# The last four frequencies turned inside SBUF, 15 late products behind the last stage, and the io ring in another room

## The chip, the core and the metric

The kernel runs on one core of one Trainium2 chip, in float32 (some operands of the dense products split into two fp32r halves). The metric is the device time of one execution in microseconds (us). Before the change the median of three runs is 531.04 us (530.05 to 533.01). The profiled execution is one more execution, 531.73 us long.

## The reference

Two branches over the same 2048 rows of 512 channels are mixed by a gate for each row. The first is a long convolution of `u` with a kernel K that is built from 128 complex modes for each channel (S4), done by Fourier transforms; the second is a dense layer with GELU and a second dense layer. Cut to what is computed:

```python
g = sigmoid((u * gate_w).sum(-1, keepdims=True))
P = exp(logdA[:, :, None] * l)                  # l = 0..2047
K = einsum("dn,dnl,dn->dl", Cc, P, dB).real
Y = rfft(pad(u)) * rfft(pad(K))                 # along the 2048 rows, padded to 4096
a = irfft(Y)[:2048] + u * Dskip
b = gelu(x @ w1 + b1) @ w2 + b2                 # 512 -> 1792 -> 512
out = g * a + (1 - g) * b
```

## The kernel before

The program has two parts. `front()` runs from 0 to about 408 us: it builds K, does the first stage of both Fourier transforms, and most of the dense layers; a planner with costs and due times sets its order. It stores the dense part of the outputs into the output tensor in DRAM (`out_dram`) from a ring of three tiles, `io`; the last two of these stores are accumulating stores on POOL's queue (L947). What is left of the second dense layer, 14 triples of matmuls (42, onto two accumulators `acc` for the last two of the 16 row tiles), is handed on as the list `late`.

`conv()` is the second part, in an order written out by hand. The long transform is split as 32 x 64: 32 outer frequencies n, each with 64 inner ones in real and imaginary parts on the 128 partitions. A loop over s = 0 to 15 takes two outer frequencies at a time. In each step:

- `fetch` loads two tiles `tk` (256 KB each, eight buffers) from DRAM on SP's queue, and `load_u` the like of the signal into buffers in `attic` and `loft`;
- `product(s)` multiplies the two spectra on DVE in six instructions (L1118 to L1123) into tiles `v`;
- `signal(s+1)` and `taps(s+2)` do the second transform stage of the coming steps on PE (L1096, into `p2u` and `p2k`), and ACT copies `p2k` to `k`;
- `inverse(s)` does the first stage back on PE (L1135, into `pa`, 8 matmuls for a step);
- `turn(s)` copies `pa` to a tile `sa` (ACT, L1141, six buffers) and stores it to DRAM in `t4_d` (L1144), on SP's queue but for the last, which goes on ACT's. An `sa` tile has 128 partitions in the order (q, i, c): 32 values of q, two halves i, real and imaginary c. With the eighth frequency of a group the whole group is loaded back into `t3` (L1153), turned so that the frequencies lie along the partitions: groups 0 to 2 in four loads of 512 KB each on POOL's queue, the last one in eight of 256 KB, four on ACT's and four on SP's;
- for s = 6 to 13 `dense(s-6)` loads 512 KB of the dense part of the output back into SBUF (L1163, SP).

In SBUF each tile has its room, and a tile that takes a room over waits for what used it last. `t3`, `tk`, `v` and the rest of `conv()` lie in rooms that `front()` used.

Behind the loop stand the remaining late products (`rest`, L1174 to L1176; one triple stands ahead of the last inverse), a warm matmul (L1212), two sums of the late accumulators into the outputs on DVE (L1216), and the last stage: 128 matmuls `pb` from `t3` (L1224), of which each pair of row tiles m = 0 to 7 takes 16. The gated sum into the output tile is done on DVE (L1235, eleven tiles) or on ACT and POOL (L1232, L1233, five tiles), and the output tiles are stored (L1237 one tile, L1239 two).

Of the kernel before, what the change touches and what calls it, by code (L numbers as in the profile page):

```python
# [9 lines left out]
F32 = mybir.dt.float32  # L10
# [62 lines left out]
N_PASS = 20  # L73
N_LATE = 2

N_ATTIC, N_LOFT, N_TK = 11, 8, 8
N_US = N_ATTIC + N_LOFT
W_DVE = ((1, 0), (3, 0), (5, 0))

GROUP = 8  # L80

ASIDE = (2, 4, 7, 9, 12)
# [24 lines left out]
def constants():  # L107
# [26 lines left out]
    f2 = np.zeros((32, 2, 64, 64))  # L134
    g2 = np.zeros((32, 64, 64, 2))
    for n, k in enumerate(ko):
        er, ei = om(4 * (q[:, None] * k + 32 * np.outer(q, k1)) + q[:, None])
        f2[n, 0], f2[n, 1] = er, -ei
        er, ei = om(4 * (qn[None] * k + 32 * np.outer(k1, qn)) + qn[None])
        g2[n, :, :, 0], g2[n, :, :, 1] = er, -ei  # L140
    f2 = f2.reshape(8, 4, P, 64).transpose(0, 2, 1, 3).reshape(8, P, 256)
# [149 lines left out]
def gated_mix(  # L291
# [23 lines left out]
    dt_d = dr.tile([1, D], F32, name="dt_d")  # L315
    t4_d = dr.tile([4, 2, 2, GROUP, 32, D], F32, name="t4_d")
    tu_d = dr.tile([2, 32, 2, 64, D // 2], F32, name="tu_d")
# [30 lines left out]
    def front(pool, psum, keep, attic, loft):  # L348
# [3 lines left out]
        def tiles(n, shape, nm, dtype=F32, space=pool):  # L352
            return [space.tile(shape, dtype, name=f"{nm}{k}") for k in range(n)]
# [25 lines left out]
        y = pool.tile([P, 2, 64, CW], F32, name="y")  # L379
        xc = tiles(2, [P, 2, 32, CW], "xc")  # L380
        xt_, xv_ = (loft[:, k * 1024 : k * 1024 + 1024].rearrange("p (a b c) -> p a b c", a=2, c=CW) for k in range(2))
        tt = loft[:, 2048:4160].rearrange("p (a b c) -> p a b c", a=2, c=CW)
# [19 lines left out]

        io = tiles(N_IO, [P, D], "io")
        gs = pool.tile([P, 16], F32, name="gs")
# [650 lines left out]
    def conv(pool, ps, late, attic, loft):  # L1055
# [17 lines left out]
        def matrices(m):  # L1073

            cc = c4s[m]
            f = cc[:, 0].rearrange("p (n k) -> p n k", n=4)
            f1 = pool.tile([P, 4, 64], F32, tag="f1", name=f"f1{m}", bufs=2)
            g = cc[:, 1].rearrange("p (s q c) -> p s q c", s=2, c=2)
            g1 = pool.tile([P, 2, 64, 2], F32, tag="g1", name=f"g1{m}", bufs=2)
            nc.scalar.mul(f1[0:64], f[64:128], -1.0)  # L1080
            nc.scalar.copy(f1[64:128], f[0:64])
            nc.scalar.mul(g1[:, :, :, 0], g[:, :, :, 1], -1.0)
            nc.scalar.copy(g1[:, :, :, 1], g[:, :, :, 0])
            mats[m] = (f, f1), [z.rearrange("p s q c -> p s (q c)") for z in (g, g1)]

# [51 lines left out]
        def turn(s):  # L1137

            for n in (2 * s, 2 * s + 1):
                sa = sas[n % 6]  # L1140
                nc.scalar.copy(sa, pas.pop(n))  # L1141
                g, k = divmod(n, GROUP)
                on = nc.sync if n < 31 else nc.scalar
                on.dma_start(t4_d[g, :, :, k].rearrange("i c q d -> q (i c) d"), sa)  # L1144
                if k < GROUP - 1:
                    continue
                rows = t4_d[g].rearrange("i c k q d -> (i c k) q d")


                w = 8 if n < 31 else 4  # L1150
                for h in range(0, 32, w):
                    on = nc.gpsimd if n < 31 else (nc.scalar, nc.sync)[h // w % 2]
                    on.dma_start(t3[g:P:4, h : h + w], rows[:, h : h + w])  # L1153

# [34 lines left out]
        for s in range(16):  # L1189
# [16 lines left out]
            if 6 <= s < 14:  # L1206
                dense(s - 6)
        rest(14)

        warm = ps.tile([P, D], F32, tag="pa", name="warm", bufs=2)  # L1210
        for _ in range(N_KEEP):
            nc.tensor.matmul(warm[0:64], mats[7][0][1][:, 3], zs[0], start=True, stop=True)  # L1212
        for s in range(N_LATE):
            z = mos[7][:, s]
            a = accs[NT - N_LATE + s]
            nc.vector.scalar_tensor_tensor(z, a, gate[:, 1, 14 + s : 15 + s], z, ALU.mult, ALU.add)  # L1216

        for m in range(8):
            tag, n = ("pa", 2) if m % 3 == 2 else ("pu", 4)
            pbs = [ps.tile([P, D], F32, tag=tag, name=f"pb{m}{i}", bufs=n) for i in range(2)]  # L1220
            for b in range(4):
                for i in range(2):
                    r = slice(64 * i, 64 * i + 64)
                    nc.tensor.matmul(  # L1224
                        pbs[i][32 * b : 32 * b + 32], g1t[r], t3[r, 4 * m + b], start=True, stop=True
                    )
            for i in range(2):
                t = 2 * m + i
                z, g = mos[m][:, i], gate[:, 0, t : t + 1]
                if t in ASIDE:  # L1230
                    a = sas[ASIDE.index(t)]
                    nc.scalar.mul(a, pbs[i], g)  # L1232
                    nc.gpsimd.tensor_add(z, z, a)  # L1233
                else:
                    nc.vector.scalar_tensor_tensor(z, pbs[i], g, z, ALU.mult, ALU.add)  # L1235
                if m in (0, 7):
                    (nc.sync, nc.scalar)[i if m else 0].dma_start(ov[m, :, i], z)  # L1237
            if 0 < m < 7:
                nc.sync.dma_start(ov[m], mos[m])  # L1239

    ctx.enter_context(tc.manual_schedule())
# [76 lines left out]
```

## Time and profile before

| | us |
|---|---|
| median of three runs | 531.04 (530.05 to 533.01) |
| the profiled execution | 531.73 |
| its span | 529.9 |
| PE busy | 502.9 (95%) |
| DVE busy | 425.5 (80%) |
| ACT busy | 348.2 (66%) |
| POOL busy | 47.5 (9%) |
| first product of `conv()` on DVE starts at | 416.54 |
| first `pb` matmul starts at | 512.97 |

The span reaches from the first to the last instruction of the profiled execution; the execution's own time is 1.83 us longer. A busy engine is one that executes an instruction; the time that DMA transfers take is not in these rows, but in a share of the 16 DMA engines and in the time from a transfer's issue to its landing. In a timeline row the bracket at the end tells how long the engine stood idle before it, and what released it. Where a row stands for several instructions (x4), its second number is the time from the first one's start to the last one's end.

### The profile page before, as it was taken

What the parts mean: (1) busy time and instruction counts of PE and PEld (TensorE: products, weight loads), DVE (VectorE), ACT (ScalarE), POOL (GpSimd) and SP (SyncE); (2) the same over time, 40 slices, a digit from 0 to 9 for tenths busy, and PEclk for the clock granted to TensorE, in tenths of its full rate; (3) what the DMA queues carried; (4) which work ended last, traced back from release to release, by engine and by line L of the source; (5) the groups of instructions that cost most, each with busy time, mean ns of one, the idle gap of its engine ahead of it and who ended that gap; (6) DMA issues with size and microseconds to landing.
All of it is one profiled execution on the core that took longest, in us unless ns stands there. A gap on an engine that the chain in (4) does not pass through costs nothing.

```text
span 529.9 us, 11252 instructions
## 1 busy us (share of the span) xinstructions
PE 502.9 (95%) x4426; PEld 348.7 (66%) x4426; DVE 425.5 (80%) x790; ACT 348.2 (66%) x539; POOL 47.5 (9%) x90
## 2 busy tenths in 40 slices
PE   8998999999999889999999999899999899999992
PEld 4776788778787666788787787688777233333360
DVE  5899999989999897899999896999801467666533
ACT  5899868599975976977459947666544355555311
POOL 1000000000000030002200320031101001010104
PEclk9999999999999989999999999999999899999997
DMA  8999932471499286426670533483718979999877
GB/s 228 380 349 329 352 133 82 143 236 32 145 292 296 64 248 203 164 79 175 126 180 1 155 46 41 111 209 42 186 47 216 287 254 299 382 406 386 324 274 294
DMA packets 90836, 108.60 MB, mean 205 GB/s; under 512 B 39056, under 2 KB 58576, under 8 KB 90144
## 3 DMA queue, kind: packets, MB, share of 16 engines
q1 hardware_dynamic: 82944, 87.67, 50.1%
q0 software_dynamic: 7360, 18.65, 14.2%
q10 hardware_dynamic: 480, 1.57, 0.8%
q8 instruction: 35, 0.57, 0.5%
q14 instruction: 17, 0.14, 0.1%
HBM read 62.25 MB, written 45.62 MB: 204 GB/s over the span
## 4 chain that ended last, share of the span: by engine, by line
PE 38%; DVE 22%; DMA 16%; issue 8%; ACT 8%; SPq 5%; POOL 1%; POOLq 0%; ACTq 0%; DVEq 0%
PE pa L1135 6%; PE p2u L1096 5%; PE p2k L1096 4%; DMA tk_d<-sk 4%; PE pz L707 4%; PE ph L876 4%; PE ph L877 3%; PE ph L878 3%; DMA tu_d<-attic 3%; PE acc L922 3%; SPq L746 3%; DVE loft L517 3%; DVE y L671 3%; DVE loft L516 3%; PE acc L923 2%
## 5 line engine op out<-in xcount | busy, mean ns | idle before, releaser
L876 PE MATMUL ph<-xh,wh 128*128 128x512 f32 x224 | 89.2, 398 | 2.9 <-ACT io L895 2.1
L922 PE MATMUL acc<-wh,hh 128*128 128x512 f32 x210 | 85.4, 406 | 3.9 <-ACT acc L928 3.9
L877 PE MATMUL ph<-xlo,wh 128*128 128x512 f32 x224 | 87.6, 391 | 0.4 <-DVE xlo L810 0.4
L878 PE MATMUL ph<-xh,wl 128*128 128x512 f32 x224 | 87.4, 390 | 0.0
L923 PE MATMUL acc<-wl,hh 128*128 128x512 f32 x210 | 82.2, 391 | 0.0
L924 PE MATMUL acc<-wh,hl 128*128 128x512 f32 x210 | 82.1, 391 | 0.0
L707 PE MATMUL pz<-y,xc 128*32 128x64 f32 x2048 | 62.5, 291 | 5.3 <-ACT attic L451 2.5
L707 PEld LDWEIGHTS pz<-y,xc 128*32 128x32 f32 x2048 | 57.1, 137 | 12.4 <-ACT sk L727 3.7
L904 DVE TENSOR_TENSOR hl<-io,hh 128x512 fp32r<-128x512 f32 x56 | 38.4, 685 | 27.2 <-ACT hh L896 27.2
L895 ACT ACTIVATE io<-ph,b1t 128x512 f32<-128x512 f32 x56 | 38.6, 689 | 26.0 <-PE ph L878 23.3
L876 PEld LDWEIGHTS ph<-xh,wh 128*128 128x128 f32 x224 | 42.0, 188 | 17.2 <-ACT io L895 3.4
L922 PEld LDWEIGHTS acc<-wh,hh 128*128 128x128 f32 x210 | 39.4, 187 | 21.1 <-issue 8.4
L877 PEld LDWEIGHTS ph<-xlo,wh 128*128 128x128 f32 x224 | 42.1, 188 | 9.4 <-DVE xlo L810 1.1
L878 PEld LDWEIGHTS ph<-xh,wl 128*128 128x128 f32 x224 | 42.1, 188 | 9.0
L924 PEld LDWEIGHTS acc<-wh,hl 128*128 128x128 f32 x210 | 39.4, 188 | 9.1 <-DVE hl L904 0.5
L671 DVE TENSOR_TENSOR y<-y,ea 128x64 f32<-128x64 f32 (+4 forms) x80 | 45.0, 563 | 0.2
L923 PEld LDWEIGHTS acc<-wl,hh 128*128 128x128 f32 x210 | 39.5, 188 | 7.3
L936 ACT ACTIVATE io<-acc,gate 128x512 f32<-128x512 f32 x30 | 20.6, 687 | 29.5 <-PE acc L924 28.7
L516 DVE TENSOR_TENSOR loft<-xc,zz 128x256 f32<-128x256 f32 (+2 forms) x48 | 37.1, 772 | 3.3 <-ACT xc L642 3.1
L1118 DVE TENSOR_TENSOR v<-p2u,k 128x512 f32<-128x512 f32 x16 | 11.1, 691 | 34.5 <-ACT sa L1141 23.6
L684 DVE TENSOR_TENSOR y<-y,loft 128x2048 f32<-128x2048 f32 x16 | 36.6, 2285 | 0.9 <-ACT loft L634 0.8
L517 DVE TENSOR_TENSOR loft<-xc,zz 128x256 f32<-128x256 f32 (+2 forms) x48 | 37.0, 771 | 0.0
(139 smaller groups left out, 845.2 us busy)
## 6 DMA issues: line engine op xcount, KB each, us to landing
tu_d<-attic SPq DMA_DIRECT2D x16, 512.0 KB, 5.9
tk_d<-sk SPq DMA_DIRECT2D x16, 512.0 KB, 6.5
tk<-tk_d SPq DMA_DIRECT2D x32, 256.0 KB, 6.0
t_d<-sa SPq DMA_DIRECT2D x31, 256.0 KB, 5.1
t<-t_d POOLq DMA_DIRECT2D x12, 512.0 KB, 7.1
attic<-tu_d SPq DMA_DIRECT2D x22, 256.0 KB, 4.6
attic<-in_xt_dram SPq DMA_DIRECT2D x16, 256.0 KB, 4.6
attic<-in_xl_dram SPq DMA_DIRECT2D x16, 256.0 KB, 5.1
```

Source lines behind the costliest of these rows:

```text
L516: vec(2 * m, lambda: vv.tensor_mul(t, a, br), due, [ka, *kb], [kt])
L517: vec(2 * m, lambda: vv.tensor_mul(v, a, bi), due, [ka, *kb], [kv])
L671: nc.vector.tensor_mul(both(n, 64 - 3 * n, n), both(0, 64 - n, n), an)
L707: nc.tensor.matmul(pk[32 * j : 32 * j + 32, gg // 4, gg % 4], x[:, r, :, ch], y[:, r, :, ch], start=(r == 0), stop=(r == 1), skip_group_ch ...
L876: nc.tensor.matmul(phs[q], h, xh[d], start=(d == 0), stop=False)
L877: nc.tensor.matmul(phs[q], h, xlo[d], start=False, stop=False)
L878: nc.tensor.matmul(phs[q], lo, xh[d], start=False, stop=(d == 3))
L895: nc.scalar.activation(g, phs[q], AF.Gelu_apprx_tanh, bias=b1t[:, c : c + 1])
L922: nc.tensor.matmul(a, h, wh[1][f], start=(f == 0 and u >= NSB), stop=False, skip_group_check=True)
L923: nc.tensor.matmul(a, h, wl[1][f], start=False, stop=False, skip_group_check=True)
L924: nc.tensor.matmul(a, l, wh[1][f], start=False, stop=(f == FH - 1), skip_group_check=True)
L1096: nc.tensor.matmul(out[64 * i : 64 * i + 64], w, x, start=True, stop=True)
```

## The change

It has three parts.

1. **The turn.** The constants of the inverse stage are laid out anew so that an `sa` tile has the partition order (i, c, q) instead of (q, i, c). The stores of n = 0 to 23 go to `t4_d`, with the pattern 4x32x512 in place of 32x4x512. Those of n = 24 to 27 go to a new DRAM tile `t5_d` with rows of 528 instead of 512 values, and come back in four loads of 256 KB on POOL's queue. Frequencies 28 to 31 aren't stored: one transfer each, three on SP's queue and one on ACT's, copies `sa` straight to four partitions of `t3`. The eight loads of the last group and four stores are gone.
2. **The late products.** Ahead of the last stage `rest` takes eight triples, and the others stand behind the `pb` matmuls of the last pair of row tiles; the two sums of the late accumulators stand behind them on DVE, and the two output tiles concerned are stored last, one on SP's queue and one on ACT's.
3. **The io ring.** `io` is allocated further ahead, and so lies in room that `t3` has later, no longer in the room that the first `v` tiles have.

```diff
@@ constants() @@
-    g2 = np.zeros((32, 64, 64, 2))
+    g2 = np.zeros((32, 64, 2, 2, 32))
...
-        g2[n, :, :, 0], g2[n, :, :, 1] = er, -ei
+        for i in range(2):
+            g2[n, :, i, 0], g2[n, :, i, 1] = er[:, i::2], -ei[:, i::2]
@@ gated_mix() @@
+N_FIRST = 8
+LATE = L // P - N_LATE
-    t4_d = dr.tile([4, 2, 2, GROUP, 32, D], F32, name="t4_d")
+    t4_d = dr.tile([3, 2, 2, GROUP, 32, D], F32, name="t4_d")
+    t5_d = dr.tile([2, 2, GROUP // 2, 32, D + 16], F32, name="t5_d")
@@ front() @@
         xc = tiles(2, [P, 2, 32, CW], "xc")
+        io = tiles(N_IO, [P, D], "io")
...
-        io = tiles(N_IO, [P, D], "io")
         gs = pool.tile([P, 16], F32, name="gs")
@@ matrices() @@
-            g = cc[:, 1].rearrange("p (s q c) -> p s q c", s=2, c=2)
-            g1 = pool.tile([P, 2, 64, 2], F32, tag="g1", name=f"g1{m}", bufs=2)
+            g = cc[:, 1].rearrange("p (s i c q) -> p (s i) c q", s=2, i=2, c=2)
+            g1 = pool.tile([P, 4, 2, 32], F32, tag="g1", name=f"g1{m}", bufs=2)
...
-            nc.scalar.mul(g1[:, :, :, 0], g[:, :, :, 1], -1.0)
-            nc.scalar.copy(g1[:, :, :, 1], g[:, :, :, 0])
+            nc.scalar.mul(g1[:, :, 0], g[:, :, 1], -1.0)
+            nc.scalar.copy(g1[:, :, 1], g[:, :, 0])
@@ turn() @@
-                on = nc.sync if n < 31 else nc.scalar
-                on.dma_start(t4_d[g, :, :, k].rearrange("i c q d -> q (i c) d"), sa)
+                if n >= 28:
+                    on = nc.sync if n < 31 else nc.scalar
+                    on.dma_start(t3[g + 4 * k : P : 32], sa)
+                    continue
+                to = t4_d[g, :, :, k] if g < 3 else t5_d[:, :, k, :, :D]
+                nc.sync.dma_start(to.rearrange("i c q d -> (i c) q d"), sa)
+                if n == 27:
+                    for j in range(4):
+                        rows = t5_d[j // 2, j % 2, :, :, :D]
+                        nc.gpsimd.dma_start(t3[32 * j + g : 32 * j + 16 : 4], rows)
                 if k < GROUP - 1:
                     continue
                 rows = t4_d[g].rearrange("i c k q d -> (i c k) q d")
-                w = 8 if n < 31 else 4
-                for h in range(0, 32, w):
-                    on = nc.gpsimd if n < 31 else (nc.scalar, nc.sync)[h // w % 2]
-                    on.dma_start(t3[g:P:4, h : h + w], rows[:, h : h + w])
+                for h in range(0, 32, 8):
+                    nc.gpsimd.dma_start(t3[g:P:4, h : h + 8], rows[:, h : h + 8])
@@ conv(), behind the loop @@
-        rest(14)
+        rest(N_FIRST)
...
-        for s in range(N_LATE):
-            z = mos[7][:, s]
-            a = accs[NT - N_LATE + s]
-            nc.vector.scalar_tensor_tensor(z, a, gate[:, 1, 14 + s : 15 + s], z, ALU.mult, ALU.add)
-
-        for m in range(8):
-            tag, n = ("pa", 2) if m % 3 == 2 else ("pu", 4)
+        order = [m for m in range(8) if m != LATE // 2] + [LATE // 2]
+        for k, m in enumerate(order):
+            tag, n = ("pa", 2) if k % 3 == 2 else ("pu", 4)
...
+            if k == 7:
+                rest(14)
...
-                if m in (0, 7):
-                    (nc.sync, nc.scalar)[i if m else 0].dma_start(ov[m, :, i], z)
-            if 0 < m < 7:
+                if k == 0:
+                    nc.sync.dma_start(ov[m, :, i], z)
+            if 0 < k < 7:
                 nc.sync.dma_start(ov[m], mos[m])
+        for i in range(N_LATE):
+            z, g = mos[LATE // 2][:, i], gate[:, 1, LATE + i : LATE + i + 1]
+            nc.vector.scalar_tensor_tensor(z, accs[NT - N_LATE + i], g, z, ALU.mult, ALU.add)
+            (nc.sync, nc.scalar)[i].dma_start(ov[LATE // 2, :, i], z)
```

The changed file is some lines longer: L1118 of before is L1122 of the changed kernel, L1144 is L1152, L1153 is L1161, L1163 is L1171, L1174 to L1176 are L1182 to L1184, L1216 is L1248, L1224 is L1228, L1235 is L1241, L1237 and L1239 are L1243 and L1245; L1149 is the direct turn, L1156 the load from `t5_d`.

How the change moves instructions is shown at three places. The first is SP's queue at the end of the loop, from s = 13 on: the stores of the `sa` tiles, the reloads of the output (`attic<-out_dram`), the last group and the first output stores, before:

```order
L1144 DMA t_d<-sa_4074 32x4x512
L1144 DMA t_d<-sa_4075 32x4x512
L1163 DMA attic<-out_dram 128x1024
L1144 DMA t_d<-sa_4076 32x4x512
L1144 DMA t_d<-sa_4077 32x4x512
L1144 DMA t_d<-sa_4072 32x4x512
L1153 DMA t_4086<-t_d 32x2048 x4
L1237 DMA out_dram<-loft 128x512 x2
```

and now:

```order
L1152 DMA t_d<-sa_4075 4x32x512
L1152 DMA t_d<-sa_4076 4x32x512
L1171 DMA attic<-out_dram 128x1024
L1149 DMA t_4087<-sa_4077 4x32x512
L1149 DMA t_4087<-sa_4078 4x32x512
L1149 DMA t_4087<-sa_4073 4x32x512
L1243 DMA out_dram<-loft 128x512 x2
```

The stores of n = 28 to 30 have become direct turns, the four loads behind them are gone, and all stores that are left have an outermost count of 4 where it was 32.

The second is DVE at the first product of the loop, with the waits of each instruction in brackets (a semaphore of DMASW belongs to POOL's queue, one of DMAHW to SP's or ACT's). Before:

```order
L1118 TENSOR_TENSOR v_4147<-p2u_4119,k_4112 128x512 [waits DMASW1_49,PE_49,Activation_49]
L1119 TENSOR_TENSOR v_4148<-p2u_4119,k_4117 128x512 [waits DMASW2_49,DVE_49,Activation_49]
L1120 TENSOR_TENSOR z_4078<-p2u_4122,k_4117 128x512 [waits DMAHW4_49,DMAHW5_49,DMAHW3_49,DMAHW6_49,DMAHW1_49,DMAHW7_49,DMAHW0_49,PE_49]
L1121 TENSOR_TENSOR z_4079<-p2u_4122,k_4112 128x512
L1122 TENSOR_TENSOR v_4147<-v_4147,z_4078 128x512 [waits DVE_49]
L1123 TENSOR_TENSOR v_4148<-v_4148,z_4079 128x512 [waits DVE_49]
```

and now:

```order
L1122 TENSOR_TENSOR v_4148<-p2u_4120,k_4113 128x512 [waits PE_49,Activation_49]
L1123 TENSOR_TENSOR v_4149<-p2u_4120,k_4118 128x512 [waits Activation_49]
L1124 TENSOR_TENSOR z_4079<-p2u_4123,k_4118 128x512 [waits DMAHW4_49,DMAHW3_49,DMAHW5_49,DMAHW1_49,DMAHW6_49,DMAHW0_49,DMAHW7_49,DVE_49,PE_49]
L1125 TENSOR_TENSOR z_4080<-p2u_4123,k_4113 128x512
L1126 TENSOR_TENSOR v_4148<-v_4148,z_4079 128x512 [waits DVE_49]
L1127 TENSOR_TENSOR v_4149<-v_4149,z_4080 128x512 [waits DVE_49]
```

The two waits on POOL's stores out of `io` (DMASW) are gone; the rest is as it was.

The third is the end of DVE's program: the gated sums of the last row tiles, and now the two late sums, which stood ahead of all `pb` sums before. Now:

```order
L1241 SCALAR_TENSOR_TENSOR attic<-pb_4908,gate,attic 128x512
L1241 SCALAR_TENSOR_TENSOR attic<-pb_4921,gate,attic 128x512
L1241 SCALAR_TENSOR_TENSOR attic<-pb_4922,gate,attic 128x512
L1248 SCALAR_TENSOR_TENSOR attic<-acc_4783,gate,attic 128x512
L1248 SCALAR_TENSOR_TENSOR attic<-acc_4815,gate,attic 128x512
```

On PE, behind the last of the 128 `pb` matmuls, stand five triples of late products (15 matmuls), onto the accumulator that DVE's last sum reads; the first of them are:

```order
L1228 MATMUL pb_4921<-t_4087,g1t 32x512
L1228 MATMUL pb_4922<-t_4087,g1t 32x512
L1182 MATMUL acc_4815<-wh_123,hh_144 128x512
L1183 MATMUL acc_4815<-wl_137,hh_144 128x512
L1184 MATMUL acc_4815<-wh_123,hl_151 128x512
```

Before, `pb` matmuls ended PE's program, and these products stood ahead of them.

More of the change, by code (lines that the diff above doesn't have):

```diff
@@ L1077, in matrices @@
             f1 = pool.tile([P, 4, 64], F32, tag="f1", name=f"f1{m}", bufs=2)
-            g = cc[:, 1].rearrange("p (s q c) -> p s q c", s=2, c=2)
-            g1 = pool.tile([P, 2, 64, 2], F32, tag="g1", name=f"g1{m}", bufs=2)
+            g = cc[:, 1].rearrange("p (s i c q) -> p (s i) c q", s=2, i=2, c=2)
+            g1 = pool.tile([P, 4, 2, 32], F32, tag="g1", name=f"g1{m}", bufs=2)
             nc.scalar.mul(f1[0:64], f[64:128], -1.0)
             nc.scalar.copy(f1[64:128], f[0:64])
-            nc.scalar.mul(g1[:, :, :, 0], g[:, :, :, 1], -1.0)
-            nc.scalar.copy(g1[:, :, :, 1], g[:, :, :, 0])
-            mats[m] = (f, f1), [z.rearrange("p s q c -> p s (q c)") for z in (g, g1)]
+            nc.scalar.mul(g1[:, :, 0], g[:, :, 1], -1.0)
+            nc.scalar.copy(g1[:, :, 1], g[:, :, 0])
+            mats[m] = (f, f1), [z.rearrange("p (s i) c q -> p s (i c q)", s=2) for z in (g, g1)]
         fac, pus, prod, pas = {}, {}, {}, {}
```

## The prediction

> **What bounds the kernel now.** I read the page first, then windows of the convolution stage (from 408 us on), then the timeline at its two ends, and last the chain of waits between them.
>
> ```profile
> span 529.9 us, 11252 instructions
> q1 hardware_dynamic: 82944, 87.67, 50.1%
> q10 hardware_dynamic: 480, 1.57, 0.8%
> t_d<-sa SPq DMA_DIRECT2D x31, 256.0 KB, 5.1
> t<-t_d POOLq DMA_DIRECT2D x12, 512.0 KB, 7.1
> t<-t_d ACTq DMA_DIRECT2D x4, 256.0 KB, 5.2
> ```
>
> The profiled execution took 531.73 us, its span 529.9, so 1.83 us lie around the span; the median of the three runs, 531.04, is 0.69 below this execution. All sums below go by the span, and take +1.83 and −0.69 at the end. The whole page says little of the stage that is changed, so here are windows of it. Columns: start:end, length, busy us of PE, PEld, DVE, ACT, POOL with counts, granted clock, DMA share of 16 engines, GB/s.
>
> ```profile
> 408.00:513.00 105.00, 101.88 (x435) 37.63 (x434) 60.45 (x98) 47.55 (x98) 7.92 (x14) 0.98 0.93 324
> 471.00:477.00 6.00, 6.00 (x30) 1.89 (x26) 4.18 (x8) 3.77 (x9) 1.65 (x4) 1.00 1.08 423
> 447.00:490.00 43.00, 43.00 (x192) 13.67 (x188) 29.47 (x48) 22.82 (x48) 4.14 (x8) 1.00 1.03 382
> 420.00:425.00 5.00, 4.17 (x12) 1.41 (x14) 4.97 (x9) 1.74 (x4) 0.00 (x0) 0.66 0.71 230
> ```
>
> From 408 to 513 us TensorE is busy 101.88 of 105 us, and the 16 DMA engines 93% of the time: **two resources are full at once**, DVE (58%) and ACT (45%) are not. From 447 to 490 PE has no idle time at all and the DMA share reads 1.03. The transfers keep up, with nothing to spare. One DMA engine moves 423/(16 × 1.08) = 24.5 GB/s in the second row, 382/(16 × 1.03) = 23.2 in the third. So 256 KB (262144 bytes) cost 0.67 us on each engine if 16 share them, 2.67 us on each if four do.
>
> The chain shows the two ends of the stage: the first steps, then what releases the last stage.
>
> ```profile
> 409.93 8.99 DMA tk<-tk_d
> 420.83 3.48 PE pa L1135 x8
> 428.04 1.92 PE pa L1135 x8
> 429.96 1.87 PE p2u L1096 x8
> 431.83 1.72 PE p2k L1096 x8
> ...
> 503.14 0.60 ACT sa L1141
> 503.74 0.02 issue
> 503.76 4.84 DMA t_d<-sa
> 510.50 5.25 DMA t<-t_d
> ```
>
> A steady step of the loop is 1.92 + 1.87 + 1.72 = 5.5 us of PE. At the end the last turned frequency is stored (4.84 us), reloaded (5.25 us), and PE fills that time with late dense products:
>
> ```profile
> 502.88 0.50 PE L1174 MATMUL acc<-wh,hh 128*128 128x512 f32 x1
> ...
> 511.65 0.39 PE L1176 MATMUL acc<-wh,hl 128*128 128x512 f32 x1
> 511.96 1.07 PE L1212 MATMUL warm<-z,f 128*64 128x512 f32 x2
> 512.97 7.17 PE L1224 MATMUL pb<-t,g1t 64*32 64x512 f32 x128
> ```
>
> 39 of them run from 502.88 to 511.96, 0.233 us apart; the last stage pb starts at 512.97, call it T.
>
> **The change part by part.** First the start.
>
> ```profile
> 416.54 0.69 DVE L1118 TENSOR_TENSOR v<-p2u,k 128x512 f32<-128x512 f32 x1 [10.25 <-DMA out_dram<-io]
> 418.29 0.69 DVE L1119 TENSOR_TENSOR v<-p2u,k 128x512 f32<-128x512 f32 x1 [1.05 <-DMA out_dram<-io]
> 417.25 1.06 PE L1096 MATMUL p2k<-tk,f 128*64 128x512 f32 x3
> 420.83 1.77 PE L1135 MATMUL pa<-v,cc 64*128 64x512 f32 x4 [2.51 <-DVE v L1122]
> ```
>
> DVE stands 10.25 us, and again 1.05, for two accumulating stores out of io, because product(0)'s v tiles lie in io's room. With io elsewhere these waits go. PE then doesn't stand 2.51 us before the first inverse, and this inverse, 3.48 us at a granted clock of 0.66 (window 420 to 425), takes its usual 1.92. **Gain 2.51 + 1.56 = 4.07 us**, if nothing else is late there. Next late would be the tk loads: the one issued at 409.93 takes 8.99 us and lands at 418.92 (the chain hands it to DVE's third product, but that one only follows the second without a gap); the taps of the second step need it when the first inverse and the second signal are through, at about 418.3 + 1.9 + 1.9 = 422. The wait of g1t's load on PE is over by 408 us, since the hidden and output products that read io's old room have ended, and costs nothing.
>
> Second, the layout of sa. ACT's copies of the sines keep their size, one 128x128 tile, and cost nothing new; PE multiplies by constants in another column order, equal in number. What changes is the pattern of the 28 stores that remain, 32x4x512 before and 4x32x512 now: the same 128 rows of 2 KB, but the outermost count falls from 32 to 4. The four direct turns and the four t5 loads have an outermost count of 4 too. No row of before has such a transfer, so I bound it. Queue q10 holds six transfers of 256 KB, one store and one output of 128 rows each and four reloads of 32: 384 rows, and 480 − 384 = 96 = 6 × 16 further packets. Every transfer there ends on 16 engines, whether it has 32 rows or 128. All have outermost counts of 32 or 128, which fall into 16 equal shares. **Low end:** the new ones are shared the same way, 0.67 us an engine, and cost nothing. **High end:** a transfer is shared along its outermost count only; four shares then go to four engines, the same four each time, 2.67 us each, while twelve rest. By bytes and row length the stores of before are nearest, which speaks for the low end; by the count that can be cut, no row stands near, and splitting the second count as well is nothing that a row shows. I take the high end as the likelier. [...]
>
> On those four engines, in 256 KB units: 28 stores gain 2.67 − 0.67 = 2.0 us each, +56.0; four stores of n = 28 to 31 go, −2.7; eight reloads of the last group go, −5.4; four direct turns come, +10.7; four t5 loads on POOL's queue come, spread as widely as a mean of one unit shows, +2.7. **Sum +61.3 us.** The window of 105 us has 7% of DMA time free, 7.4 us, and takes that off: **+53.9**. Nothing else hides it: PE needs tk and u from the same engines, sa has six buffers, so ACT's copies, the pa and v tiles and DVE's products wait in turn behind the stores. The 4.07 us of the start vanish in it, since the engines, not PE, set the pace. T becomes 512.97 + 53.9 = 566.9.
>
> Third, the end.
>
> ```profile
> 512.07 0.75 DVE L1216 SCALAR_TENSOR_TENSOR attic<-acc,gate,attic 128x512 f32<-128x512 f32 x1 [4.01 <-PE acc L1176]
> 514.15 2.73 DVE L1235 SCALAR_TENSOR_TENSOR loft<-pb,gate,loft 128x512 f32<-128x512 f32 x4 [1.32 <-PE pb L1224]
> 516.79 5.09 DVE L1235 SCALAR_TENSOR_TENSOR attic<-pb,gate,attic 128x512 f32<-128x512 f32 x7
> 496.62 1.46 SPq L1144 DMA_DIRECT2D t_d<-sa  x2
> 522.65 1.14 SPq L1237 DMA_DIRECT2D out_dram<-attic  x1
> out_dram<-loft SPq DMA_DIRECT2D x2, 256.0 KB, 2.5
> out_dram<-attic SPq DMA_DIRECT2D x1, 256.0 KB, 6.0
> ```
>
> Before, the last store leaves at 522.65, lands 6.0 us later, and the span ends 1.25 after that: T + 16.9. By the order of instructions 15 products, not 18, now stand behind pb (the other three had already been taken ahead of it in both). PE is through with them at T + 7.17 + 15 × 0.233 = T + 10.7, and the last one's result is there 0.39 − 0.23 = 0.2 later; DVE's eleven pb sums end at T + 8.9, so the products cost DVE a wait, and the last late sum ends at T + 10.9 + 0.75 = T + 11.6. Its store leaves 0.1 later, lands after 3.2 (my value between 2.5 for a store alone and 6.0 behind others, nearer the former, as the large outputs have drained by then), and with 1.25 behind it the span ends at **T + 16.2**, 0.7 earlier than before. What goes from ahead of pb, 15 × 0.233 = 3.5 us, is worth more than that only if PE and not the loads sets T. The first pb product now waits for all four direct turns and all four t5 loads at once, since every partition of t3 gets rows from each; the turns of n = 28 to 30 and the tk loads stand ahead of the last turn on SP or its engines, and pb waits behind all.
>
> With the DMA engines as the bound PE waits often, and the granted clock falls as at 420: I add the 1.56 us of one such stretch. Sum: 566.9 + 16.2 + 1.6 = 584.7, +1.83 − 0.69 = **586 us** (rounded).
>
> [...]
>
> **The rivals.** *B, faster: the new patterns are still shared by 16 engines.* For it speaks that rows, bytes and queue are those of the stores of before. Then the last inverse ends 4.07 us earlier, at 502.97 − 4.07 = 498.9; the 24 products left take 5.6, the warm one 1.0: PE is ready at 505.5. The last sa copy ends at 503.74 − 4.07 = 499.7, the last direct turn is issued then and lands 4.8 later, like the store at 503.76, at 504.5. The stores of n = 26 and 27 are the two of the row at 496.62; the second, issued at 498.08 − 4.07 = 494.0, lands after 5.1, at about 499, and the t5 loads behind it take up to the 7.1 us of the POOL reloads of twice their size: 506. So T ≈ 506.5. The end is 506.5 + 16.2 = 522.7, +1.1: **524 us**.
>
> *A, slower: the forecast.* Its one mechanism is the sharing among four engines, its place every store from 424 us on, its price 2.0 us a store. It decides once the 28 stores add more than the 7.4 us of free DMA time and the 7 us that B gains, that is above 0.51 us a store; eight sharing engines, 0.67 us more, would already do it. Its own range: 586 − 12 (the engines give the 1.08 share of the second window: 159/1.08 = 147) − 8 (the direct turns over 16 engines, 4 × 2.0) = 566; upward 23.2 GB/s instead of 24.5 add 9, and three direct turns at twice their price 8: 602.
>
> *C, no change: a new wait takes the place of the old one.* tk lands too late for the first steps, or the eight loads ahead of pb land together only 4 us after the PE is ready. B's 7 us shrink to 1 to 3: 528 to 530 us. The row at 409.93 speaks against it, with 3 us in hand.
>
> *D, little: four engines, but other ones each time.* The load stays even, single landings lengthen from 5.1 by 2.0 us, and the stage keeps its pace: 524 + 2 to 4, about 527.
>
> **How the numbers follow.** A measurement of this kernel can tell about 0.5% (2.7 us) from no change. A 0.64, and 0.01 for slower in other ways; B 0.26; C 0.05; D 0.04. Within 0.5% are C and a piece of D: 0.06. Faster is B and the rest of D: 0.29. Slower 0.65. The likeliest case's own range is 566 to 602; as A alone holds too little, the range reaches to B and takes its 524 in with 2 us below: 522 to 602.
>
> **What would show it.** For A: PE's idle time between 424 and 560 us, put down to DMA tk, t_d or sa; a step of over 8 us instead of 5.5; landings of t_d<-sa near 10 us and more with the DMA share far under 0.93 at the same time; first pb near 567; T to the end about 16. For B: PE without idle time after the first inverse, DMA share near 1, pb at 506 to 507. In both: no wait of DVE's first product on out_dram<-io, and 15 acc products behind the last pb with two sums of DVE behind them. Wrong would be the start's gain if DVE's first product then waits for tk or u, and the end if pb's wait names POOL's t5 loads long after the direct turns have landed.

## The result and the profile after

The changed kernel takes 586.43 us (median of four runs, 585.86 to 589.24) against 531.49 us of the kernel before, run beside it (530.05 to 533.01): a ratio of 1.104, 95% interval 1.100 to 1.109. It is **slower by 55 us**; forecast was 586 us. The profiled execution is the longest of the four, 589.24 us, with a span of 587.5.

The page of the changed kernel, the rows that answer to those of before:

```profile
span 587.5 us, 11242 instructions
...
q1 hardware_dynamic: 82380, 86.62, 45.0%
q0 software_dynamic: 8448, 19.70, 13.2%
q10 hardware_dynamic: 276, 0.52, 0.2%
```

The packets show **how many engines carried a narrow transfer**. Beyond its rows a transfer on these queues had further packets, called end packets here: before, 96 = 6 x 16 for the six on q10. Queue q10 (ACT's) now holds one direct turn and one output, 128 rows each: 276 − 256 = 20 = 16 + 4 end packets, 16 for the output and 4 for the turn. On q1 (SP's), 31 stores of 128 + 16 packets and four reloads of 32 + 16 gave way to 28 stores and three turns: with four end packets each that is 31 x 144 + 4 x 48 − 31 x 132 = 564 fewer, and 82944 − 82380 is 564. That there is one end packet for each engine fits the share of the engines: from 543 to 547 us, with transfers of SP's queue alone under way, it is 0.26, four of 16 engines.

Windows of the loop in the changed kernel, columns as before:

```profile
408.00:450.00 42.00, 41.44 (x180) 14.27 (x180) 25.88 (x43) 21.74 (x45) 1.72 (x2) 1.00 0.76 235
450.00:520.00 70.00, 51.05 (x180) 16.48 (x178) 27.33 (x45) 22.15 (x46) 4.12 (x8) 0.88 0.66 236
```

Up to 450 us PE is nearly always busy: SP had issued twelve `tk` loads by 418 us. Then PE stands for 19 of 70 us, while the DMA engines are 66% busy on the mean, with 236 GB/s where it was 382: transfers bound the loop, but not all 16 engines. The waits of the same kernel from 408 to 570 us (who waited, for what: us in total, times, longest), and the durations of the issues of the stores (ns: shortest, median, longest):

```profile
ACT sa L1145 <- DMA t_d<-sa: 33.9, 10, 6.9
...
PE pb L1228 <- DMA t<-sa: 21.5, 1, 21.5
...
PE p2k L1100 <- DMA tk<-tk_d: 19.5, 5, 7.5
...
L1152 SPq DMA_DIRECT2D t_d<-sa x28: 511/1202/5164, 422.7 to 530.1; - x28
```

ACT waits for an `sa` buffer that isn't stored yet, PE for `tk` tiles, and SP itself stands at the stores (median 1.2 us for an issue, 0.53 before). PE's timeline at the start of the loop, over its slow part and at the last stage:

```profile
420.10 1.13 PE L1139 MATMUL pa<-v,cc 64*128 64x512 f32 x4
...
453.92 1.13 PE L1139 MATMUL pa<-v,cc 64*128 64x512 f32 x4
...
515.35 1.13 PE L1139 MATMUL pa<-v,cc 64*128 64x512 f32 x4
...
565.24 1.88 PE L1228 MATMUL pb<-t,g1t 64*32 64x512 f32 x2 [21.55 <-DMA t<-sa]
568.11 9.58 PE L1228 MATMUL pb<-t,g1t 64*32 64x512 f32 x126 [0.99 <-DMA t<-t_d]
577.62 0.50 PE L1182 MATMUL acc<-wh,hh 128*128 128x512 f32 x1
```

The first inverse starts without a wait and takes its usual time: the start's gain is there. Between the inverses at 453.92 and 515.35 lie six steps of 10.2 us each, where there were 5.5. The first two matmuls of the last stage start at 565.24 (forecast 566.9), after PE stood 21.55 us for a direct turn; the other 126 start at 568.11, and the 15 late products follow them. The chain that ended last reaches these 126 by another way:

```profile
516.98 33.28 DMA t_d<-sa x2
...
551.39 2.10 POOL t L1156 x3
553.49 9.18 issue
562.67 5.31 DMA t<-t_d
568.11 9.58 PE pb L1228 x126
```

The last stores land at 550.3, POOL issues its four loads of the padded tile behind them, the fourth 9.18 us after the third, and that one lands 2.7 us after PE's wait for the direct turns had ended. So the stores, the turns and these loads together set the last stage.

### The profile page after: what moved, and what is told of

It is laid out like the page before. It is cut to its first block, busy times and chain, and to the rows that moved or that the text cites. A ratio compares the mean times of both kernels' runs of the same rounds, so it can differ in the third digit from the quotient of the medians.

```text
span 587.5 us, 11242 instructions
## 1 busy us (share of the span) xinstructions
PE 524.8 (89%) x4426; PEld 357.8 (61%) x4426; DVE 425.7 (72%) x790; ACT 348.7 (59%) x539; POOL 50.3 (9%) x94
## 3 DMA queue, kind: packets, MB, share of 16 engines
q1 hardware_dynamic: 82380, 86.62, 45.0%
## 4 chain that ended last, share of the span: by engine, by line
PE 53%; DMA 20%; ACT 10%; issue 6%; DVE 6%; SPq 2%; POOL 1%; DVEq 0%; ACTq 0%; POOLq 0%
PE pz L711 7%; DMA tk<-tk_d 7%; DMA t_d<-sa 6%; PE acc L926 5%; PE ph L880 5%; PE ph L881 5%; PE ph L882 5%; PE p2k L1100 5%; PE acc L927 5%; PE acc L928 5%; PE pa L1139 3%; PE p2u L1100 3%; DMA tk_d<-sk 2%; PE pz L429 2%; SPq L750 2%
## 5 line engine op out<-in xcount | busy, mean ns | idle before, releaser
L926 PE MATMUL acc<-wh,hh 128*128 128x512 f32 x210 | 86.8, 413 | 5.4 <-ACT acc L932 5.4
L927 PE MATMUL acc<-wl,hh 128*128 128x512 f32 x210 | 83.5, 398 | 0.0
L711 PEld LDWEIGHTS pz<-y,xc 128*32 128x32 f32 x2048 | 57.0, 136 | 10.2 <-ACT sk L731 3.3
L1122 DVE TENSOR_TENSOR v<-p2u,k 128x512 f32<-128x512 f32 x16 | 11.1, 691 | 61.2 <-PE p2u L1100 31.9
L1145 ACT COPY sa<-pa 128x512 f32<-128x512 f32 x32 | 18.0, 587 | 51.2 <-DMA t_d<-sa 33.9
L1100 PE MATMUL p2k<-tk,cc 128*64 128x512 f32 x64 | 24.9, 664 | 19.5 <-DMA tk<-tk_d 19.5
L520 DVE TENSOR_TENSOR loft<-xc,zz 128x256 f32<-128x256 f32 (+2 forms) x48 | 37.1, 773 | 4.3 <-ACT xc L646 4.2
```

The costliest lines, as they stand in the source:

```text
L520: vec(2 * m, lambda: vv.tensor_mul(t, a, br), due, [ka, *kb], [kt])
L711: nc.tensor.matmul(pk[32 * j : 32 * j + 32, gg // 4, gg % 4], x[:, r, :, ch], y[:, r, :, ch], start=(r == 0), stop=(r == 1), skip_group_ch ...
L926: nc.tensor.matmul(a, h, wh[1][f], start=(f == 0 and u >= NSB), stop=False, skip_group_check=True)
L927: nc.tensor.matmul(a, h, wl[1][f], start=False, stop=False, skip_group_check=True)
L1100: nc.tensor.matmul(out[64 * i : 64 * i + 64], w, x, start=True, stop=True)
```

## The experiments

Each ratio is to the kernel before, run beside the experiment on the same chip (medians 530.8 to 531.9 us).

**The moved ring alone** (before, `io` allocated where the change puts it).

```diff
         xc = tiles(2, [P, 2, 32, CW], "xc")
+        io = tiles(N_IO, [P, D], "io")
...
-        io = tiles(N_IO, [P, D], "io")
```

> The kernel before with the io ring moved and nothing else. Theory 1 (the narrow stores cost the time, and the start's wait is a real gain of its own): 4.1 us faster than before, 527.4 us against 531.5, the first inverse starting 2.5 us earlier against the products ahead of it and taking 1.9 us. Theory 2 (the moved ring brings a new wait, so the loss has to do with it): 531 us or more.

528.27 us, ratio 0.995 (0.992 to 0.998): 2.7 us faster, with an interval from 1.3 to 4.1. In the timeline DVE's first product waits for PE's `p2u`, no longer for a store:

```profile
416.43 0.69 DVE L1118 TENSOR_TENSOR v<-p2u,k 128x512 f32<-128x512 f32 x1 [6.08 <-PE p2u L1096]
```

By the clock of the profile this is no earlier than before (416.54), because `front()` ended 4.0 us later in this execution: its last product starts at 411.93, before at 407.89. From there the first inverse starts 10.3 us later, where it was 12.9, and takes 1.92 us instead of 3.48, together 4.2 us. The gain is real; of the forecast 4.1, which the trace shows, the medians show 2.7, and 4.1 is the upper end of their interval.

**Parts 2 and 3 without part 1** (the changed kernel with the constants, stores and reloads of before).

```diff
-                if n >= 28:
-                    on = nc.sync if n < 31 else nc.scalar
-                    on.dma_start(t3[g + 4 * k : P : 32], sa)
-                    continue
...
+                on = nc.sync if n < 31 else nc.scalar
+                on.dma_start(t4_d[g, :, :, k].rearrange("i c q d -> q (i c) d"), sa)
```

> The changed kernel with the turn of before (constants, stores, reloads): parts 2 and 3 of the change alone. Theory 1 (the whole loss lies in the patterns of part 1): 526 to 528 us, 4 from the start, and little from the end, where the reload of the last group sets the first product of the last stage at about 510. Theory 2 (the late products behind the last stage, or the ring, lose time themselves): 531 us or more.

527.45 us, ratio 0.995 (0.992 to 0.998). The whole loss lies in part 1, and this kernel is faster than both the kernel before, by about 0.5%, and the changed one; none of the other runs is measurably faster than this one.

**The pattern of the stores alone** (before, with the new column order, all 32 frequencies stored as 4x32x512 and reloaded as before).

```diff
-                on.dma_start(t4_d[g, :, :, k].rearrange("i c q d -> q (i c) d"), sa)
+                on.dma_start(t4_d[g, :, :, k].rearrange("i c q d -> (i c) q d"), sa)
```

> The kernel before with the column order of the constants and the pattern of all 32 stores changed to 4x32x512, and nothing else: no direct turn, no loads from the padded tile, io ring and late products as before. Theory 1 (a store with four outermost counts occupies four engines, always the same, for 2.67 us instead of 16 for 0.67): 32 x 2.0 = 64 us added on these four, 7.4 us of free time taken off, 1.6 for a cold clock: 589 us, from 575 to 600. Theory 2 (the loss belongs to the direct turns, the wait of the last stage, or the moved instructions): 531 to 535 us.

587.47 us, ratio 1.108 (1.103 to 1.113). **One changed pattern is as slow as the whole change**, with no direct turn in the kernel. Its packets:

```profile
q1 hardware_dynamic: 82572, 87.67, 46.0%
q0 software_dynamic: 7360, 18.65, 12.7%
q10 hardware_dynamic: 468, 1.57, 0.7%
```

82944 − 82572 = 372 = 31 x 12 on SP's queue, 480 − 468 = 12 on ACT's: each store lost 12 of 16 end packets, with the same bytes. The profile doesn't name the DMA engines, but it counts them: in the changed kernel, from 543 to 547 us, with narrow transfers of SP's queue alone under way, the share of the 16 engines is 0.26, that is four engines, at 98 GB/s, or 2.7 us for 256 KB. From 548 to 553 us ACT's direct turn runs beside them, and the share stays at 0.26, 13.8% for SP's queue and 12.2% for ACT's, at 101 GB/s. SP's queue alone had 26.3% before: the two share four engines, as each would keep its own pace on a four of its own.

**The wide stores back, the direct turns kept** (the hybrid: the new column order only for n = 28 to 31).

```diff
+NEW_TURN = (7,)
...
-                nc.sync.dma_start(to.rearrange("i c q d -> (i c) q d"), sa)
+                nc.sync.dma_start(to.rearrange("i c q d -> (i c) q d" if n // 4 in NEW_TURN else "i c q d -> q (i c) d"), sa)
```

> The changed kernel with the new column order for the last four frequencies alone; those of 0 to 27 are stored with 32 outermost counts as before, to the same places. Four direct turns and four loads remain narrow. Theory 1 (28 narrow stores are nearly all of the loss): 523 to 527 us, faster than the kernel before. Theory 2 (the direct turns or the joint wait of the last stage are a large part): over 540 us.

541.68 us, ratio 1.020 (1.016 to 1.024). The time lies in theory 2's range, but each theory had a part: 44.8 us of the loss are gone with the 28 narrow stores, and the kernel is still 14.2 us above the one with the old turn, and slower than before. PE and SP in the timeline at the end of this kernel, and a step of its chain of waits:

```profile
505.84 1.07 PE L1230 MATMUL warm<-z,f 128*64 128x512 f32 x2
521.53 9.85 PE L1238 MATMUL pb<-t,g1t 64*32 64x512 f32 x128 [14.62 <-DMA t<-sa]
...
497.71 3.34 SPq L1159 DMA_DIRECT2D t<-sa  x3
...
500.52 20.88 DMA t<-sa
```

The loop runs at full pace, and PE is ready at 506.9. The last direct turn then takes 20.88 us to land; the first of the four was issued at 497.7. From there to the last landing are 23.7 us, 5.9 for each of the four, where the prediction had 2.67. Not all of it is the turns' own: the DMA share from 485 to 500 us is still 0.92, and POOL's loads of the padded tile run beside the turns.

Two runs ask why a direct turn is that slow. **Each turn cut into four pieces of one partition**, from the hybrid:

```diff
-                    on.dma_start(t3[g + 4 * k : P : 32], sa)
+                    for b in range(4):
+                        on.dma_start(t3[g + 4 * k + 32 * b : g + 4 * k + 32 * b + 1], sa[32 * b : 32 * b + 32])
```

> The hybrid with each direct turn cut into four transfers into one partition each (32x512 from 32 partitions). What is disputed are the 14 us by which the hybrid is above the kernel with the old turn. Theory E (a direct turn is slow because four engines carry it, 2.67 us a turn): spread over 16 engines the turns cost 0.67 each, and the time falls to 524 to 528 us. Theory W (a turn is slow because it writes only four partitions, whatever number of engines carries it): no gain, 540 us or more, since each piece now writes a single partition.

543.37 us, ratio 1.022 (1.018 to 1.026): no gain. That the pieces were carried by 16 engines is in the packets, and what these did in a window of the wait:

```profile
q1 hardware_dynamic: 82896, 86.62, 49.7%
...
505.00:520.00 15.00, 0.62 (x2) 0.00 (x0) 0.00 (x0) 0.00 (x0) 0.67 (x1) 0.62 0.93 108
```

The hybrid has 82716 packets on q1; 180 more are 12 pieces with 16 end packets less three turns with 4. In these 15 us the 16 engines are 93% occupied and move 108 GB/s, POOL's loads of the padded tile included, where before the loop moved 382 at a share of 1.03: they are held up. What is left in common with the uncut turns is the four partitions written, and that the copy stays inside SBUF; no run copies inside SBUF to more partitions, so these two are not told apart.

**All eight frequencies of the last group turned directly**, without the padded tile and its loads:

```diff
-NEW_TURN = (7,)
+NEW_TURN = (6, 7)
...
-                if n >= 28:
+                if n >= 24:
...
-                if n == 27:
-                    for j in range(4):
-                        rows = t5_d[j // 2, j % 2, :, :, :D]
-                        nc.gpsimd.dma_start(t3[32 * j + g : 32 * j + 16 : 4], rows)
```

> The hybrid with all eight frequencies of the last group turned directly, and no store or load of the padded tile. Theory E (four engines carry a turn, 2.67 us each, 21 us for eight, begun at about 483): they are through at 505 to 510 and the time is 526 to 531 us. Theory W (a turn takes about 5.2 us, as four of the hybrid took from 497.7 to 521.4 together): eight take 42 us from about 483 on, the last stage starts at 522 to 527, and the time is 541 to 547 us. If the loads on POOL's queue were what held the last stage in the hybrid, it would be under 530 us too.

552.13 us, ratio 1.039 (1.034 to 1.044). SP's turns in the timeline, the last two waits of the chain, and a window of PE's wait:

```profile
488.31 1.35 SPq L1158 DMA_DIRECT2D t<-sa  x2
...
495.09 10.52 SPq L1176 DMA_DIRECT2D attic<-out_dram  x1
505.70 12.56 SPq L1158 DMA_DIRECT2D t<-sa  x3
...
489.09 19.62 DMA t<-sa
...
511.56 21.28 DMA t<-sa
...
510.00:520.00 10.00, 0.00 (x0) 0.00 (x0) 0.00 (x0) 0.00 (x0) 0.00 (x0) 0.51 0.26 78
```

Eight turns run from 488.3 to 532.8, 5.6 us each on the mean. Theory E is out, and the time is over the range of theory W too: the turns began 5 us later than I had put them. But 5.6 us aren't the price of a turn by itself. SP stood 10.5 us at a reload of the output and issued its last three turns only from 505.7 on, and POOL's loads of the group before, 2 MB, were issued from 489.5 on (the share is 0.84 from 490 to 500 us). From 510 to 520 us, with little but turns under way, four engines are busy (0.26 of 16) and move 78 GB/s: 3.4 us for 256 KB, between the 2.67 of E and the 5.2 of W. The delay doesn't need the loads of the padded tile, since there are none of them here.

**Stores cut in four, on 16 engines** (the changed kernel, each store as four transfers of 32 rows).

```diff
-                nc.sync.dma_start(to.rearrange("i c q d -> (i c) q d"), sa)
+                for b in range(4):
+                    on = nc.sync
+                    on.dma_start(to[b // 2, b % 2], sa[32 * b : 32 * b + 32])
```

> The changed kernel with each of the 28 stores cut into four transfers of 32 rows of 2 KB, one for each (i, c): same column order, bytes, rows and places in DRAM, only the outermost count is 32. Theory 1 (the number of engines that share a store makes the loss of the loop): the loop goes back to 5.5 us a step and the time to that of the hybrid, 541.7 us, up to 8 more if SP's issues (8 stores, 2 to 5 others of 0.5 us each in a step) set the pace: 540 to 550. Theory 2 (the new order of columns or places itself makes the transfers slow): 580 us or more.

567.27 us, ratio 1.065 (1.059 to 1.071): 19 us come back, not the 45 of the hybrid. The cut does put 16 engines to work: q1 has 84060 packets, 1680 = 28 x (64 − 4) more than in the change. In the timeline SP issues without a pause, one step's four rows here:

```profile
427.72 4.93 SPq L1154 DMA_DIRECT2D t_d<-sa  x8
432.75 0.91 SPq L350 DMA_DIRECT2D tk<-tk_d  x2
433.71 0.97 SPq L345 DMA_DIRECT2D attic<-tu_d  x2
434.78 5.01 SPq L1154 DMA_DIRECT2D t_d<-sa  x8
```

From 427.72 to 434.78 are 7.1 us, more than PE's 5.5: the issues look like a new bound. So the next run moves half of them.

**Cut stores on two queues** (the kernel of the run before, two of each four on ACT's).

```diff
-                    on = nc.sync
+                    on = (nc.sync, nc.scalar)[b % 2]
```

> As the run with the stores cut in four, but two of each four go on ACT's queue. Open is why the cut stores gave 567 us and not the hybrid's 541.7. Theory S (SP's issues set the pace there: its period of a step in the trace is 7.3 us, 8 stores 5.0 and the loads 2.3, against the 5.5 of PE): SP now needs 4.8 us a step, and the time is 541 to 547 us. Theory 2 (the cut stores or their order still cost DMA time): 560 us or more.

576.06 us, ratio 1.088 (1.079 to 1.096): my explanation of the 567 us failed this test, at least in this form. ACT's issues now stand between its own copies, and PE waits for those (waits of this kernel, 408 to 545 us):

```profile
PE p2k L1100 <- ACT f L1085: 24.1, 6, 8.5
```

The cut stores on ACT cost PE 24 us that way. Whether they'd be free on a queue with room is open.

**The narrow stores on POOL's queue.**

```diff
-                nc.sync.dma_start(to.rearrange("i c q d -> (i c) q d"), sa)
+                nc.gpsimd.dma_start(to.rearrange("i c q d -> (i c) q d"), sa)
```

> The changed kernel with the 28 narrow stores issued on POOL's queue in place of SP's; pattern and bytes as in the change. Theory 1 with the same four engines each time on SP's queue, other ones by turns on POOL's: the load is even again, single landings stay long, 541 to 556 us with a DMA share near 0.9 in the loop. Theory 2 (a transfer of this pattern is slow wherever it runs, or POOL's takes the same four): 580 us or more.

581.58 us, ratio 1.094 (1.089 to 1.099), beyond what I expected of even load. Its waits and a window of its loop:

```profile
POOL t_d L1152 <- issue: 48.8, 7, 16.2
...
424.00:450.00 26.00, 26.00 (x114) 8.17 (x112) 17.25 (x29) 13.55 (x28) 4.19 (x7) 1.00 0.91 266
```

The share of 0.91 fits transfers that are spread over more than four engines, but POOL then stands 48.8 us ahead of its issues, for nothing that the profile shows, and the stores behind it come late. The run itself doesn't decide the question it was made for. The trace of the changed kernel says more: from 555 to 558 us, with three narrow loads of POOL's queue and SP's last turns under way, the share is 0.74, twelve engines, 0.55 of it POOL's queue and 0.20 SP's, while from 545 to 550 us, with narrow transfers of SP's and ACT's queues alone, it is 0.26. POOL's narrow loads were carried by more engines than those four.

**A dose: stores cut in two, an outermost count of 2.**

```diff
-                nc.sync.dma_start(to.rearrange("i c q d -> (i c) q d"), sa)
+                for i in range(2):
+                    nc.sync.dma_start(to[i], sa[64 * i : 64 * i + 64])
```

> The changed kernel with each of the 28 stores cut in two, one for each i: an outermost count of 2. Theory 1 (a transfer is shared along its outermost count by that many engines, always the same lowest ones): 256 KB on two engines cost 5.35 us each, 4.68 more than on 16; 28 x 4.68 = 131, plus 10.7 + 2.7 - 8.1 as in the prediction, less 7.4: 129 us on the two busiest engines in place of 53.9, so 586.4 + 75 = 661 us, from 640 to 680. Theory 2 (a share of four comes from something else, or the two halves run on different engines): within 10 us of the change, 577 to 597 us.

659.86 us, ratio 1.243 (1.235 to 1.250), 1 us from the 661 that follow from two engines. This is the clearest test of the first theory: twice as many transfers, the same bytes, and half as many engines add 73 us. Queue q1 has 82380 packets, as many as in the change: 56 stores with two end packets each, where 28 had four. Which engines carry them, the lowest or others, the profile doesn't say.

**More late products ahead of the last stage** (parts 2 and 3 with `N_FIRST = 11`, then 12). With eight, PE stands 2.1 us before the last stage:

```profile
506.73 9.91 PE L1222 MATMUL pb<-t,g1t 64*32 64x512 f32 x128 [2.10 <-DMA t<-t_d]
```

```diff
-N_FIRST = 8
+N_FIRST = 11
```

> The kernel with the old turn, but eleven triples ahead of the last stage in place of eight. With eight PE stands 2.1 us before the last stage, and its 128 matmuls take 9.9 us at a lower granted clock in place of 7.2. Three triples more fill 2.1 us. If the idle time is what lowers the clock, the last stage takes 7.2 to 7.6 again, two triples stay behind it, and the time is 522.5 to 525.5 us, 2 to 5 below the 527.45 of the old turn with eight. If the clock falls anyway, 526 to 528.

> As with eleven, with twelve triples ahead: PE is 0.7 us past the landing of the loads, one triple stays behind. 523 to 526 us if idle time lowers the clock; 526 to 528 if not.

527.70 us (ratio 0.994, 0.990 to 0.997) and 528.00 us (0.995, 0.992 to 0.998): the same as with eight, within their intervals. With eleven, the last stage and the time around it:

```profile
508.26 7.54 PE L1222 MATMUL pb<-t,g1t 64*32 64x512 f32 x128 [0.69 <-DMA t<-t_d]
...
508.00:520.00 12.00, 9.04 (x134) 3.60 (x134) 9.02 (x13) 3.44 (x5) 6.27 (x5) 1.00 0.94 359
```

The clock stays at 1.00 (with eight it is 0.83 from 507 to 517 us) and the stage is 2.4 us shorter, as expected of it, but the end isn't earlier by that: from the stage's start on the DMA engines are 94% busy with 4 MB of output, and from the issue of the last output store on SP's queue to the end of the span are 7.5 us (518.68 to 526.2), where it was 6.6 with eight (519.08 to 525.7). So the stores and no longer PE set the end.

## Why the prediction was right

**The bound.** Two resources full at once (PE 101.88 of 105 us, DMA share 0.93), little room for transfers: right. The new bound is the one named, and the time came out within 1 us. That is nearer than the sum deserves, as its terms show.

**The start.** The wait on `io`'s stores is gone, nothing else was late, and alone it is worth 2.7 us (1.3 to 4.1) of the forecast 4.07. That it vanishes in the loop of the changed kernel, as written, no run shows by itself.

**The stores: 2.0 us each on four engines.** Shown by five things together: 4 end packets in place of 16; four engines busy, at 2.7 us for 256 KB, when narrow transfers alone are under way; the pattern alone gives 587 us (589 expected); with wide stores 44.8 us return; with two engines the time is 660 (661 expected). The pace agrees too. A step took the engines 1.03 x 5.5 = 5.67 us, of which two wide stores 1.33; two narrow ones put 5.33 in their place, 9.67 us, and six steps of the loop took 10.2 each. Ahead of the result no run showed that a transfer is shared along its outermost count; it was the author's choice between two values. That SP's and ACT's queues use the same four is seen in the share, which stays at 0.26 with both under way, while SP's part of it falls to 0.14. The sum's 2.7 us for the four t5 loads take them as spread over all engines, which no run of before shows either; three of them kept 0.55 of the engines busy, about nine, beside SP's turns.

**The direct turns: 2.67 us each. This term was mis-sized.** From the first issue to the last landing a turn took 5.6 to 5.9 us, but other transfers are in that. With little else under way, four engines carried turns at 78 GB/s, 3.4 us each, in the run with eight (510 to 520 us), and two turns in the changed kernel at 102 GB/s, 2.6 us each (550.3 to 552.2 us); narrow transfers of SP's queue went at 98 GB/s, 2.7 us (543 to 547 us). What the rest of the 5.6 to 5.9 us is made of, the runs don't tell. More engines didn't help: with the turns cut for 16 engines the time is 543.37 us, with uncut ones 541.68. That the four partitions written are the limit would be an estimate: no run tells them apart from the copy's staying inside SBUF. Twice the price, with which the range's upper end counts three turns, is an estimate as well; the 5.6 to 5.9 us are about that, with the other transfers in them.

The sum also had the turns in a wrong place. It counted them as work of the engines beside the loop, but they can only start when the last inverses are done, and PE then waits for them: in the hybrid, whose loop runs at full pace, 14.62 us.

**Luck.** These errors didn't show in the total, because others lay against them. Counted in this order of parts, turns and loads cost 14.2 us (from the old turn's 527.45 to the hybrid's 541.68) in place of 5.3, and the stores 44.8 (from there to the change's 586.43) in place of 48.6 (56.0 less 7.4): 59.0 in place of 53.9. Parts 2 and 3 gained 3.5 us (530.93 to 527.45), where the sum has a loss of 0.9 (1.6 less 0.7). That the total came out within 1 us is luck; that the stores cost some 45 us of it is not.

**Rival B** (16 engines still share) fell, and its 524 us were wrong even in its own case: the hybrid with cut turns has 16 engines for every store and every turn, and takes 543.4. Its step "the last direct turn is issued then and lands 4.8 later" took a store over 128 partitions for the price of a write into four; in the hybrid it took 20.88. **C** is right in one half: no new wait replaced the one on `io`, but PE did wait for the turns and loads ahead of the last stage, 14.62 us in the hybrid where C had 4. **D** saw nothing: on SP's and ACT's queues the load isn't even (share 0.26).

**The end.** Fifteen products behind the last stage, and DVE's two sums behind them, as forecast. From the block of 126 `pb` matmuls at 568.11 to the end of the span are 19.4 us, against 16.2 + 1.6; after the wait these 126 took 9.58 us, not 7.17 plus 1.56 for 128. Moving the products is worth nothing that can be measured: parts 2 and 3 give 527.45, part 3 alone 528.27, with overlapping intervals.

## What to carry to other kernels

Look at the outermost count of each transfer, ahead of its bytes: a store of 256 KB with 32 outermost rows and one with 4 look alike in the source, and here, where the DMA engines were full (share 1.03 from 447 to 490 us), the second cost four times as much on a quarter of them (2.67 us for 0.67, at 24.5 GB/s an engine), and 28 such stores 44.8 us. On SP's and ACT's queues the number of packets, less the rows, told how many engines a transfer had (16 end packets or 4), and the DMA share told it where such transfers ran alone (0.26). A copy that skips a trip through DRAM isn't cheap for that: the four turns into four partitions each made PE wait 14.62 us in the hybrid. Measure such a copy before you price it like a store, and ask who waits for it.

## What the runs showed of the hardware

- Transfers of 256 KB with an outermost count of 4 had four end packets, where those with 32 had 16, and kept four engines busy (share 0.26) at 98 GB/s on SP's queue; those of 128 KB with a count of 2 had two. With narrow transfers of SP's and ACT's queues under way at once the share stayed at 0.26, while three loads of POOL's queue and the last turns kept twelve busy (0.74).
- Copies of 256 KB inside SBUF into four partitions 32 apart went at 78 GB/s (3.4 us) on four engines with little else under way in one run, and at 102 GB/s (2.6 us) in another. Cut into pieces of one partition for 16 engines, four of them took 25.4 us (496.5 to 521.9) beside POOL's loads; the engines counted as 93% busy at 108 GB/s, where the loop of before had 382 GB/s at a share of 1.03. The busy share alone didn't tell there whether engines worked or waited.
- POOL stood 9.2 us ahead of the last of its four loads from the padded tile in the change, and up to 16.2 us ahead of a store where it issued the stores, each time for nothing that the profile shows.
- With 2.1 us of idle time before it, the last stage of 128 matmuls took 9.9 us at a granted clock of 0.83, with 0.7 us 7.5 at 1.00: but the kernel was no faster for it (527.45 and 527.70 us).
